# Attention with an MLP behind it: normalised rows of six batches transposed by DMA on ScalarE's queue instead of by TensorE

## The chip, the cores and the metric

One Trainium2 chip, one of its cores. The metric is the device time of one execution in microseconds; lower is better. It is given as the median of three runs.

## What is computed

Two stages, batch by batch. `q`, `k`, `v` are 8 batches x 8 heads x 576 rows x 64, `s` is 8 x 8 x 576.

```python
scores = scale * (q @ k.T) + min(-(cum[:, None] - cum[None, :]), 0)   # cum = cumsum(max(s, 0))
attn = softmax(where(causal, -1e9, scores))
x = (attn @ v), heads side by side                                    # 8 x 576 x 512
xn = (x - mean) / sqrt(var + 1e-6) * g_ln
out = x + max(xn @ w_ch1, 0) @ w_ch2                                  # 512 -> 2048 -> 512
```

## The kernel before, in words

The order of the work is written out by hand: every engine runs its instructions in program order, and the framework adds the semaphore waits that the data needs. The main loop runs over n = 0 to 63, one **slot** for each head h = n % 8 of each batch b = n // 8 (lines 745 to 834). The MLP is a `queue` of small **units** that the slots take from with `run_units`, so that TensorE has matmuls to do while other engines work on the attention.

A slot of the steady part (n from 16) does this, in this order:

- `pre(n)` (line 675): loads ahead. For batches 3 to 7, keys and queries come as rows: `ld_rows` (SP), `cast_rows` to bf16 with the bias columns beside them (POOL), and `tr_rows` (SP, line 186), a DMA transpose of up to 128 x 1024 elements into `kq`. For each half batch (4 heads) there are five `tr_rows`, issued by SP two, two and one in the slots h = 0, 1, 2 for the heads 4 to 7 of the batch and h = 4, 5, 6 for the heads 0 to 3 of the next. `ld_v` (SP, line 139) loads `v` of the next batch in slots h = 1 to 5, and `cast_v` (POOL) casts it a slot later.
- `scores(b, h)` (line 304): matmuls into three PSUM banks `sa`, `sb`, `sc` (pool `ps_s`, three buffers), and for each an exp on ScalarE into `er`; then four causal selects on POOL. The next slot's scores need those banks, so they wait for these exps. Even heads add `scores_d`.
- `run_units(1, True)`, `run_units(1)`, then `pv_next()`: the product with `v` for the head two slots before, and on VectorE its scaling into `xb` (and, for the last 64 rows, `xm`). In slot h = 1 it also finishes batch b - 1: `ln_open`, and `ln_xn` for each tile t, which writes a normalised tile `xn` (128 x 512, bf16; line 451). Tiles 0 to 3 are the batch's first 512 rows; tile 4 exists for odd batches only, and holds the last 64 rows of two batches.
- `ln_tr(b - 1, t)` for t = 0, 1 in slot h = 2 and t = 2, 3, 4 in slot h = 3: four TensorE transposes with the identity into PSUM (`trx`, line 484) and a copy by VectorE (by ScalarE for batch 1) into `xT`, or for tile 4 into `xTm`.
- the rest of the slot's units. At the end of slot h = 3 what is left of the queue is run and `batch_units(b - 1)` joins it: 16 units `mlp1` (line 493: four matmuls of 512 columns, then a relu into `hT`, by VectorE for the first unit of a slot and by ScalarE for the others), then 16 units `mlp2` (line 511: four matmuls each; four units finish one row tile, VectorE forms `yo` at line 524, and SP stores it at line 542). `nu` spreads them, four to a slot.

`ph` and `py` of the MLP share the pool `ps_m` with two buffers, `yo` has three, `xn` five, `xT` two (one for each of two batches).

After the loop comes a tail: the last two `pv`, the tiles of batch 7 one by one (`ln_xn`, a unit, `ln_tr` with a copy by ScalarE), the rest of batch 6's units, batch 7's units, and `mixed_units` for the 512 rows in `xm`.

The lines that the change and the working touch most:

```python
lt = {2: (0, 1), 3: (2, 3, 4)}.get(h, ()) if b > 1 else ()
for t in lt:
    ln_tr(b - 1, t, "act" if b == 2 else "dve")
    if t != 1 and t != 4:
        run_units(1)
        nu -= 1
...
if b > 1 and h == 3:
    run_units(len(queue))
    queue += batch_units(b - 1)
```

Of the kernel before, what the change touches and what calls it, by code (L numbers as in the profile page):

```python
# [15 lines left out]
P = 128  # L16
# [3 lines left out]
def kernel(  # L20
# [11 lines left out]
    nc = tc.nc  # L32
    B, H, S, D = q.shape
# [5 lines left out]
    NF = S // P  # L39
# [48 lines left out]
    xTm = const.tile([P, KD, 512], BF16, name="xTm")  # L88
# [7 lines left out]
    def copy_on(eng, out, in_):  # L96
        if eng == "act":
            nc.scalar.copy(out=out, in_=in_)  # L98
        elif eng == "dve":
            nc.vector.tensor_copy(out=out, in_=in_)  # L100
        else:
            nc.gpsimd.tensor_copy(out=out, in_=in_)  # L102
# [140 lines left out]
    def tr_pair(g):  # L243
        tr_kind("k", g)
        tr_kind("q", g)
# [58 lines left out]
    def scores(b, h):  # L304
        e = er[:, h % 4, :]
        pe_mask = b * H + h < NM

        def bank(name, blocks, o):
            a = ps_s.tile([P, 512], F32, name=name, tag="s")
            for c, kb, q0, q1, diag in blocks:  # L310
                for a0, a1, cols in q_cols(b, h, q0, q1):
                    nc.tensor.matmul(  # L312
                        a[:, c + a0 - q0 : c + a1 - q0],
                        lhsT=k_cols(b, h, kb),
                        rhs=cols,
                        start=True,
                        stop=not (pe_mask and diag),
                    )
                if pe_mask and diag:
                    nc.tensor.matmul(  # L320
                        a[:, c : c + P], lhsT=ident, rhs=maskT, start=False, stop=True
                    )
            nc.scalar.activation(out=e[:, o : o + 512], in_=a, func=ACT.Exp, scale=scale)  # L323

        bank("sa", ((0, 0, 0, 512, True),), 0)
        bank("sb", ((0, 0, 512, 576, False), (64, 1, 128, 576, True)), OB)
        bank("sc", ((0, 2, 256, 576, True), (320, 3, 384, 576, True)), OC)
        if pe_mask:
            return
        for o in (0, OB + 64, OC, OC + 320):  # L330
            nc.gpsimd.affine_select(  # L331
                out=e[:, o : o + P],
                in_=e[:, o : o + P],
                compare_op=ALU.is_ge,
                fill=0.0,
                base=0,
                pattern=[[1, P]],
                channel_multiplier=-1,
            )
# [70 lines left out]
    def x_tiles(b):  # L410
        ts_ = [xb[b][:, t, :] for t in range(NF)]
        if b % 2 == 1:
            ts_.append(xm[b // 2])
        return ts_
# [13 lines left out]
    xTs = {}  # L428
    xns = {}
# [5 lines left out]
    def ln_rstd(b):  # L435
        n = len(x_tiles(b))
        rs = rstd[:, b, 0:n]
        nc.vector.tensor_scalar_add(out=rs, in0=mvs[b][:, 0:n, 1], scalar1=1e-6)  # L438
        nc.gpsimd.tensor_tensor(out=rs, in0=rs, in1=mhalf[:, 0:n], op=ALU.pow)  # L439

    def ln_aggr(b, t):
        nc.vector.bn_aggr(out=mvs[b][:, t, :], in_=st[b][:, t, 0 : 4 if b == 0 else 3, :])

    def ln_xn(b, t):
        tiles = x_tiles(b)
        if t >= len(tiles):
            return
        if b > 0:
            ln_aggr(b, t)
        xn = xnp.tile([P, Dm], BF16, name="xn", tag="xn")  # L450
        nc.vector.scalar_tensor_tensor(  # L451
            out=xn,
            in0=tiles[t],
            scalar=mvs[b][:, t, 0:1] if b > 0 else mean0[:, t : t + 1],
            in1=gb,
            op0=ALU.subtract,
            op1=ALU.mult,
        )
        xns[b, t] = xn
        if b > 0 and t == len(tiles) - 1:  # L460
            ln_rstd(b)
# [16 lines left out]
    def ln_tr(b, t, eng="dve"):  # L478
        if (b, t) not in xns:
            return  # L480
        xn = xns.pop((b, t))
        tr = ps_t.tile([P, KD, P], BF16, name="trx", tag="tr")
        for kd in range(KD):
            nc.tensor.transpose(tr[:, kd, :], xn[:, kd * P : (kd + 1) * P], ident)  # L484
        if t < NF:
            dst = xTs[b][:, :, t * P : (t + 1) * P]
        else:
            dst = xTm[:, :, (b // 2) * P : (b // 2 + 1) * P]
        copy_on(eng, dst, tr)

    first_unit = [False]

    def mlp1(xT, fb):
# [63 lines left out]
    def run_units(n, dve_first=False):  # L557
        for i in range(n):
            if queue:
                first_unit[0] = dve_first and i == 0  # L560
                queue.pop(0)()
# [33 lines left out]
    for i in range(2):  # L595
# [5 lines left out]
        out=maskT,  # L601
        in_=maskT,
# [18 lines left out]
    for t in range(NT):  # L621
# [5 lines left out]
        out=c_in, in0=c_in, scalar1=0.0, scalar2=1.0 / scale, op0=ALU.max, op1=ALU.mult  # L627
    )
    nc.vector.tensor_tensor_scan(
        out=c_sc, data0=c_one, data1=c_in, initial=0.0, op0=ALU.mult, op1=ALU.add  # L630
# [114 lines left out]
    for n in range(BH):  # L745
        b, h = n // H, n % H
        pre(n)
        if n < 8:
            scores(b, h)
            if h in (1, 3, 5, 6):  # L750
                scores_d(b, h // 2)
            if h in (0, 2, 4):
                qk_pair(h // 2 + 1, ("dve", "dve"), ("act", "dve" if h < 4 else "act"))
            pend.append((b, h))
            if n == 7:
                pv_next()
                tr_pair(4)
                pv_next()
                evac_pair("k", 4, ("act", "act"))
                evac_pair("q", 4, ("act", "act"))  # L760
                trc = bias_tr()
                keep_warm(8)
                continue
            if n % 2 == 1 or n == 0:
                keep_warm(2)
            if n > 1:
                pv_next()
            if n == 6:
                pv_next()
            continue  # L770
        if n == 8:

            phs = [
                pool.tile([P, 512], F32, name="ph", tag=tag)
                for pool, tag in ((ps_m, "m"), (ps_m, "m"), (ps_s, "s"), (ps_s, "s"))
            ]

            def columns(t):
                cols = slice(t * P, (t + 1) * P)
                for fb, ph in enumerate(phs):  # L780
                    for kd in range(KD):
                        nc.tensor.matmul(  # L782
                            ph[:, cols],
                            lhsT=w1_bf[:, kd, fb * P : (fb + 1) * P],
                            rhs=xTs[0][:, kd, cols],
                            start=(kd == 0),
                            stop=(kd == KD - 1),
                        )

            for t in range(NF):  # L790
                ln_tr(0, t, "act" if t < 3 else "dve")
                if t > 0:
                    columns(t - 1)
            columns(NF - 1)
            for fb, ph in enumerate(phs):
                if fb % 2 == 0:
                    nc.scalar.activation(out=hT[:, fb, :], in_=ph, func=ACT.Relu)
                else:
                    nc.vector.tensor_scalar_max(out=hT[:, fb, :], in0=ph, scalar1=0.0)
            ln_first_rstd()  # L800
            queue += batch_units(0)[4:]
            scores(b, h)
            scores_d(b, h // 2)
            pend.append((b, h))
            run_units(1)
            continue

        end = next(m for m in (8 * i + 3 for i in range(2, B + 1)) if m >= n)
        nu = (2 if n < 16 else -(-len(queue) // (end - n + 1))) - 2
        if n in PAIRS:  # L810
            qk_pair(PAIRS[n], ("dve", "dve"), ("act", "act"))
        scores(b, h)
        run_units(1, True)
        if h % 2 == 0:
            scores_d(b, h // 2)
        run_units(1)
        if n > 9:
            pv_next()
        if n == 9:
            bias_rows(trc)  # L820
        pend.append((b, h))
        lt = {2: (0, 1), 3: (2, 3, 4)}.get(h, ()) if b > 1 else ()
        for t in lt:
            ln_tr(b - 1, t, "act" if b == 2 else "dve")
            if t != 1 and t != 4:
                run_units(1)
                nu -= 1
        if n == 2 * H + 2:
            for t in range(3, NT):
                ln_xn(1, t)  # L830
        run_units(nu)
        if b > 1 and h == 3:
            run_units(len(queue))
            queue += batch_units(b - 1)
    pv_next()
# [3 lines left out]
    for t in range(NT):  # L839
        ln_xn(B - 1, t + 1)  # L840
        run_units(1)
        ln_tr(B - 1, t, "act")
    run_units(len(queue))
    queue += batch_units(B - 1)
    queue += mixed_units()
# [30 lines left out]
```

## Time and profile before

| | |
|---|---|
| median of 3 runs | 368.11 us (367.84 to 368.29) |
| the profiled execution | 368.74 us, of which the span from first to last instruction is 367.0 us |
| TensorE busy | 357.8 us, 3079 matmuls |
| VectorE, ScalarE, POOL busy | 205.8, 194.2, 161.3 us |
| DMA transposes on SP's queue (`tr_rows`) | 50, 1274 ns in the middle from start to end of issue |
| TensorE transposes of `xn` (`trx`) | 144 |
| DMAs on ScalarE's queue | 5 stores, at the end |

In a profile line the first number is the start in us from the start of the span, the second the length in us; then the engine (PE is TensorE, ACT ScalarE, DVE VectorE, SPq SP's DMA queue), the line of the kernel, the operation, output <- input with shapes, and how many of them were merged. In brackets stands the idle time of the engine before it, and what ended that. A row for a DMA shows its issue on the queue, not its landing; landings are in the trace as events of the DMA's semaphore. In the answer for one tile the three numbers are the least, middle and greatest length in ns.

### The profile page before, as it was taken

How to read it: one execution, taken by the hardware profiler on the slowest of the kernel's cores; microseconds unless marked ns; L12 is line 12 of the kernel's file. 1: busy time of each engine (PE TensorE's matmuls, PEld its weight loads, DVE VectorE, ACT ScalarE, POOL GpSimd, SP SyncE). 2: the span in 40 equal slices, each digit the busy share in tenths (PEclk: the TensorE clock that was granted, in tenths of full speed). 3: DMA queues.
4: the chain of work that ended last, by engine and by line, in shares of the span. 5: the costliest groups of instructions: out<-in, count | busy, mean ns of one | idle time of the engine just before them, and what ended most of it. 6: DMA issues, size and time to landing. Idle time of an engine off the chain costs nothing.

```text
span 367.0 us, 8372 instructions
## 1 busy us (share of the span) xinstructions
PE 357.8 (97%) x3079; PEld 198.0 (54%) x3079; DVE 205.8 (56%) x539; ACT 194.2 (53%) x371; POOL 161.3 (44%) x441
## 2 busy tenths in 40 slices
PE   8899999999999999999999999999999999999995
PEld 3577565565555555555555555555555554444444
DVE  7597789796438453944384547743675483112211
ACT  5795988568743674357534753476337522501410
POOL 8864375747553746445754562555652101000000
PEclk9999999999999999999999999999999999999999
DMA  7999995579965989599968996798730011011013
GB/s 138 170 195 175 201 204 88 116 179 173 187 140 129 236 177 189 117 227 184 192 158 203 206 188 133 183 202 183 167 102 2 0 60 57 3 56 58 3 29 86
DMA packets 147981, 50.42 MB, mean 137 GB/s; under 512 B 134185, under 2 KB 143268, under 8 KB 147940
## 3 DMA queue, kind: packets, MB, share of 16 engines
q1 hardware_dynamic: 129364, 40.74, 50.9%
q0 software_dynamic: 18176, 8.62, 20.4%
q10 hardware_dynamic: 400, 0.52, 0.5%
q8 instruction: 24, 0.39, 0.4%
q14 instruction: 17, 0.14, 0.2%
HBM read 37.11 MB, written 9.44 MB: 127 GB/s over the span
## 4 chain that ended last, share of the span: by engine, by line
PE 85%; DVE 7%; ACT 3%; DMA 2%; issue 1%; ACTq 0%
PE ph L497 32%; PE py L515 31%; PE pot L389 7%; PE sc L312 4%; PE sa L312 3%; PE sb L312 3%; DVE xn L451 2%; PE trx L484 2%; ACT er L323 2%; DMA kq<-c 1%; ACT kq L98 1%; PE trqk L255 1%; DVE stats L423 1%; PE ph L782 1%; DMA c_in<-in_s_dram 1%
## 5 line engine op out<-in xcount | busy, mean ns | idle before, releaser
L515 PE MATMUL py<-w_bf,hT 128*128 128x512 bf16 (+1 forms) x592 | 136.5, 373 | 0.4 <-DVE yo L524 0.4
L497 PE MATMUL ph<-xT,w_bf 128*128 128x512 bf16 x496 | 117.8, 379 | 0.1
L507 ACT ACTIVATE hT<-ph 128x512 bf16<-128x512 f32 x102 | 61.0, 598 | 62.8 <-PE ph L497 62.8
L515 PEld LDWEIGHTS <-hT 128*128 128x128 bf16 x592 | 53.5, 98 | 49.1 <-issue 0.9
L497 PEld LDWEIGHTS <-w_bf 128*128 128x128 bf16 x560 | 50.3, 97 | 51.7 <-issue 3.3
L323 ACT ACTIVATE er<-sa 128x512 bf16<-128x512 f32 x64 | 38.2, 597 | 70.3 <-PE sa L312 39.9
L331 POOL TENSOR_SCALAR_AFFINE_SELECT er<-er 128x128 bf16<-128x128 bf16 x216 | 58.2, 294 | 26.4 <-ACT er L323 26.3
L505 DVE TENSOR_SCALAR hT<-ph 128x512 bf16<-128x512 f32 x38 | 26.3, 692 | 54.5 <-PE ph L497 49.1
L176 POOL CAST rows<-rowtmp 128x512 bf16<-128x512 f32 (+1 forms) x50 | 30.5, 609 | 49.1 <-DMA rowtmp<-in_q_dram 48.4
L312 PEld LDWEIGHTS <-kq 68*128 68x128 bf16 x440 | 32.8, 97 | 26.5 <-DMA kq<-c 1.6
L389 PEld LDWEIGHTS <-er 128*128 128x128 bf16 x960 | 37.4, 98 | 14.2 <-issue 0.7
L389 PE MATMUL pot<-v_bf,er 128*128 128x65 bf16 x960 | 39.6, 193 | 0.1
L323 ACT ACTIVATE er<-sc 128x512 bf16<-128x512 f32 x64 | 39.1, 610 | 0.0
L397 DVE RECIPROCAL rinv<-pot 128x5 f32<-128x5 f32 x64 | 12.3, 192 | 47.5 <-PE pot L389 47.2
L323 ACT ACTIVATE er<-sb 128x512 bf16<-128x512 f32 x64 | 38.3, 598 | 0.1
L524 DVE SCALAR_TENSOR_TENSOR yo<-py,rstd,xb 128x512 f32<-128x512 f32 x32 | 23.9, 748 | 25.5 <-PE py L515 20.8
L399 DVE TENSOR_TENSOR xb<-pot,rinv 128x256 f32<-128x256 f32 x64 | 27.2, 425 | 2.2
L439 POOL TENSOR_TENSOR rstd<-rstd,mhalf 128x4 f32<-128x4 f32 (+1 forms) x8 | 8.8, 1097 | 43.8 <-DVE rstd L438 43.8
L312 PE MATMUL sa<-kq 68*128 68x512 bf16 x64 | 24.4, 381 | 1.2 <-DMA kq<-c 1.1
L423 DVE BATCH_NORM_STATS2 stats<-xb 128x6 f32<-128x128 f32 (+2 forms) x100 | 25.3, 312 | 0.4
L312 PE MATMUL sc<-kq 68*128 68x256 bf16 (+1 forms) x208 | 25.2, 232 | 0.3
L102 POOL CAST v_bf<-vtmp 128x512 bf16<-128x512 f32 (+1 forms) x30 | 18.4, 613 | 14.3 <-DMA vtmp<-in_v_dram 14.3
(101 smaller groups left out, 332.8 us busy)
## 6 DMA issues: line engine op xcount, KB each, us to landing
out_dram<-yo SPq DMA_DIRECT2D x32, 256.0 KB
vtmp<-in_v_dram SPq DMA_DIRECT2D x24, 256.0 KB
rowtmp<-in_k_dram SPq DMA_DIRECT2D x40, 128.0 KB
rowtmp<-in_q_dram SPq DMA_DIRECT2D x40, 128.0 KB
w_bf<-in_moe_w_ch_dram POOLq DMA_DIRECT2D x8, 512.0 KB, 11.1
kp<-in_k_dram POOLq DMA_DIRECT2D x11, 144.0 KB, 6.6
qp<-in_q_dram POOLq DMA_DIRECT2D x11, 144.0 KB, 7.3
v_bf<-in_v_dram POOLq DMA_DIRECT2D x8, 128.0 KB, 8.5
```

Source lines behind the costliest of these rows:

```text
L176: nc.gpsimd.tensor_copy(out=r[0:pn, :, :, 0:D], in_=loaded.pop(("rows", gam, t))[0:pn])
L312: nc.tensor.matmul(a[:, c + a0 - q0 : c + a1 - q0], lhsT=k_cols(b, h, kb), rhs=cols, start=True, stop=not (pe_mask and diag),)
L323: nc.scalar.activation(out=e[:, o : o + 512], in_=a, func=ACT.Exp, scale=scale)
L331: nc.gpsimd.affine_select(out=e[:, o : o + P], in_=e[:, o : o + P], compare_op=ALU.is_ge, fill=0.0, base=0, pattern=[[1, P]], channel_mult ...
L389: nc.tensor.matmul(pot[:, t, :], lhsT=e[:, o : o + P], rhs=vv[:, kb, h, :], start=(kb == 0), stop=(kb == last),)
L399: nc.vector.tensor_tensor(out=xb[b][:, :, hs], in0=pot[:, 0:NF, 0:D], in1=rinv[:, 0:NF].unsqueeze(2).to_broadcast([P, NF, D]), op=ALU.mult,)
L423: nc.vector.bn_stats(out=st[b][:, t, part, :], in_=x[:, lo:hi])
L497: nc.tensor.matmul(ph, lhsT=w1_bf[:, kd, fb * P : (fb + 1) * P], rhs=xT[:, kd, :], start=(kd == 0), stop=(kd == KD - 1),)
L505: nc.vector.tensor_scalar_max(out=hT[:, fb, :], in0=ph, scalar1=0.0)
L507: nc.scalar.activation(out=hT[:, fb, :], in_=ph, func=ACT.Relu)
L515: nc.tensor.matmul(py[0], lhsT=hT[:, fb, t * P : (t + 1) * P], rhs=w2_bf[:, fb, c0:c1], start=(fb == 0), stop=(fb == FB - 1),)
L524: nc.vector.scalar_tensor_tensor(out=yo, in0=py[0], scalar=rs, in1=x[:, c0:c1], op0=ALU.mult, op1=ALU.add)
```

## The change

A new function `ln_dma(b, t)` transposes an `xn` tile by one DMA transpose, issued on ScalarE's queue, straight into `xT` or `xTm`. It takes the place of `ln_tr` for batches 2 to 7; batches 0 and 1 keep `ln_tr`. In the loop it is called at these places, for batch b - 1:

- t = 0 in slot h = 2, t = 2 in slot h = 3 and t = 4 in slot h = 5, each after `pv_next()` and ahead of the slot's remaining units;
- t = 1 in slot h = 3 and t = 3 in slot h = 4, each after `pre(n)` and ahead of `scores(b, h)`.

In the tail it replaces `ln_tr` for batch 7. The units of batch b - 1 now join the queue at the end of slot h = 4 instead of h = 3, and `end`, from which `nu` is worked out, moves by one slot with it.

```diff
--- before.py
+++ after.py
@@ -487,6 +487,16 @@
         else:
             dst = xTm[:, :, (b // 2) * P : (b // 2 + 1) * P]
         copy_on(eng, dst, tr)
+
+
+    def ln_dma(b, t):
+        if (b, t) not in xns:
+            return
+        if t < NF:
+            dst = xTs[b][:, :, t * P : (t + 1) * P]
+        else:
+            dst = xTm[:, :, (b // 2) * P : (b // 2 + 1) * P]
+        nc.scalar.dma_start_transpose(out=dst, in_=xns.pop((b, t)))
 
     first_unit = [False]
 
@@ -805,8 +815,10 @@
             run_units(1)
             continue
 
-        end = next(m for m in (8 * i + 3 for i in range(2, B + 1)) if m >= n)
+        end = next(m for m in (8 * i + 4 for i in range(2, B + 1)) if m >= n)
         nu = (2 if n < 16 else -(-len(queue) // (end - n + 1))) - 2
+        if b > 2 and h in (3, 4):
+            ln_dma(b - 1, 2 * h - 5)
         if n in PAIRS:
             qk_pair(PAIRS[n], ("dve", "dve"), ("act", "act"))
         scores(b, h)
@@ -819,17 +831,19 @@
         if n == 9:
             bias_rows(trc)
         pend.append((b, h))
-        lt = {2: (0, 1), 3: (2, 3, 4)}.get(h, ()) if b > 1 else ()
+        lt = {2: (0, 1), 3: (2, 3, 4)}.get(h, ()) if b == 2 else ()
         for t in lt:
-            ln_tr(b - 1, t, "act" if b == 2 else "dve")
+            ln_tr(b - 1, t, "act")
             if t != 1 and t != 4:
                 run_units(1)
                 nu -= 1
         if n == 2 * H + 2:
             for t in range(3, NT):
                 ln_xn(1, t)
+        if b > 2 and h in (2, 3, 5):
+            ln_dma(b - 1, {2: 0, 3: 2, 5: 4}[h])
         run_units(nu)
-        if b > 1 and h == 3:
+        if b > 1 and h == 4:
             run_units(len(queue))
             queue += batch_units(b - 1)
     pv_next()
@@ -839,7 +853,7 @@
     for t in range(NT):
         ln_xn(B - 1, t + 1)
         run_units(1)
-        ln_tr(B - 1, t, "act")
+        ln_dma(B - 1, t)
     run_units(len(queue))
     queue += batch_units(B - 1)
     queue += mixed_units()
```

## The prediction

> **What bounds the kernel now.** I read the page first, parts 1, 2 and 4: busy time, slices, the chain that ended last.
>
> ```profile
> PE 357.8 (97%) x3079; PEld 198.0 (54%) x3079; DVE 205.8 (56%) x539; ACT 194.2 (53%) x371; POOL 161.3 (44%) x441
> PE   8899999999999999999999999999999999999995
> PE 85%; DVE 7%; ACT 3%; DMA 2%; issue 1%; ACTq 0%
> ```
>
> TensorE has no slice with room in it, and the chain lies on it: a matmul taken away is time saved, a pause of TensorE is time lost. Then the answer for the tile trx, which the change removes from batch 2 on:
>
> ```profile
> L484 PE MATMUL trx<-ident,xn x144: 217/219/230, 32.1 to 303.1; 128*128 128x128 bf16 x144
> L100 DVE COPY xT<-trx x21: 403/415/425, 35.6 to 271.7; 128x512 bf16<-128x512 bf16 x21
> ```
>
> 219 ns is a latency. What four transposes cost TensorE is read from starts in the timeline; lines from slots 42 and 43 (batch 5, h = 2 and 3), and the next pair of SP's own transposes:
>
> ```profile
> 186.13 0.38 PE L312 MATMUL sa<-kq 68*128 68x512 bf16 x1
> 188.06 0.27 ACT L358 ACTIVATE er<-sd 64x128 bf16<-64x128 f32 x1
> 189.04 0.39 PE L484 MATMUL trx<-ident,xn 128*128 128x128 bf16 x4
> 189.26 1.03 PE L515 MATMUL py<-w_bf,hT 128*128 128x512 bf16 x4
> 190.02 0.74 DVE L524 SCALAR_TENSOR_TENSOR yo<-py,rstd,xb 128x512 f32<-128x512 f32 x1
> 190.79 0.36 SPq L542 DMA_DIRECT2D out_dram<-yo  x1
> 191.24 1.22 SPq L186 DMA_TRANSPOSE kq<-rows  x1
> 191.69 0.60 ACT L323 ACTIVATE er<-sa 128x512 bf16<-128x512 f32 x1 [3.36 <-PE sb L312]
> 194.78 0.51 SPq L139 DMA_DIRECT2D vtmp<-in_v_dram  x1
> 200.72 3.15 SPq L186 DMA_TRANSPOSE kq<-rows  x2
> ```
>
> The reader is to see three things. Four transposes take 189.26 - 189.04 = 0.22 us. ScalarE is done with slot 42 at 188.33 and idle for 3.36 us. And SP's transposes fall between: the one that slot 42 issues in program order starts only at 191.24, because SP stood behind a store that waited for yo, which VectorE computes after four xn.
>
> The trace's semaphore records give landings: SP's 50 transposes land 2.65 to 5.52 us after they start, median 3.38; the ten of 64 rows (as many elements as an xn tile) 2.65 to 2.94.
>
> **What the Trainium skill says.** "DMA: Bandwidth & Descriptors", section "Silent corruption: two transposing streams in flight at once": transposes issued from SP and from ACT are two streams, and the first of the later stream must wait for the full completion of the earlier. Before, only SP transposes, so no run here shows it; the forecast rests on the changed program keeping this order both ways. "Perfetto Trace Analysis", section "DMA Instruction — HWDGE (DVE, Sync)": the reported time of a DMA leaves out its semaphore wait and the movement of data. The trace agrees: 1.27 us reported, 3.38 us to landing. "TensorE: Matmul & The Clock Gate", section "What's actually happening": after an idle window of some 3.4 us the array runs at half rate. The trace agrees at the start, where 12 matmuls of 512 columns take 5.13 us (0.43 each; 0.216 later).
>
> **The change, part by part.** Slots are counted from the scores of one head to those of the next; plain ones last 4.58 or 4.63 us.
>
> Removed, TensorE: 4 full tiles for each of 6 batches and 3 mixed tiles, 27 groups of four. Slots h = 2 and 3 last 5.08 and 5.03 us (5.62 where the batch being normalised is odd), so 0.45 + 0.45 or 0.45 + 1.04 over plain ones: 3 x 0.90 + 2 x 1.49 = 5.7 us in the loop. In the tail five groups at 0.22 are 1.1. Together **-6.8 us**. The 22 copies of VectorE (415 ns) and 5 of ScalarE (587 ns) lie beside TensorE: nothing.
>
> Added, issue: 27 DMAs. No ScalarE transpose is in the trace; nearest are SP's of 64 rows, 1.22 to 1.27 us. I take 1.25, not less than the 0.5 us of a plain DMA there, not more than SP's longest 2.43. 27 x 1.25 = 34 us of ScalarE, but in slots with only exps (ScalarE busy 1.72 of 4.64 us in slot 42), so without waits it costs nothing. It cannot gain, since it only adds to the queue.
>
> Moved: the MLP chunk one slot later. Four units of 0.86 us go from the loop to the tail, where TensorE is as full: 0, within 1 us either way. It keeps tile 3's landing before its first reader, and covers the tail: eight units (6.9 us) stand between the last transposes of batch 7 and their reader.
>
> Added, waits. Behind ln_dma on ScalarE stand the exps of the next slot; behind these the next-but-one scores, which need the score banks (three, one per sa, sb, sc). I count from the start of slot h = 2.
> - T0 (tile 0) comes after SP's last row transpose of that slot. That lands at +7.7, 9.2, 7.8, 9.4, 8.3 us in batches 3 to 7; ScalarE is there at +2.2. T0 starts at the landing.
> - T1 comes next, before the exps of h = 3. Here a second wait: SP's and ScalarE's DMAs use eight semaphores in turn, and in the records none is issued before the DMA eight places back has landed (on GpSimd's eight, several are issued 0.28 us after, i.e. were waiting). Eight back from T1 is SP's v load of slot h = 2 (194.78 above), landing at +11.8, 14.2, 12.8, 13.6; batch 7 has none. T1 starts there.
> - So the exps of h = 3 start at S = T1 + 1.25: +13.1, 15.5, 14.1, 14.9 and, in batch 7, 10.8. They take 1.6 us and the scores of h = 4 end 0.4 later, at S + 2.05; undisturbed they end at 4.63 + 4.58 + 0.9 = +10.1. Stalls 5.0, 7.4, 6.0, 6.8, 2.7: **+28 us**.
> - T2 starts when those exps end. SP's two row transposes of h = 4 must wait until it lands (2.75), the second starts 1.3 later and lands after 3.3; T3, written before the exps of h = 4, waits for that; then 1.25 issue, 1.65 exps, 0.4 scores: 10.65 us, of which 5.0 are a slot in any case. 5.65 each in batches 3 to 6: **+22.6 us**. Bounds 5.2 to 7 each: the two transposes took 4.7 to 6.5 us from first start to last landing. In batch 7 SP has none left.
> - T4 (batches 4 and 6) waits likewise for SP's next pair; two relus stand behind it, about 1.2 us each: **+2.4**.
> - SP also waits for T2, T3 and T4; loads behind it slip by 3 us, which the longer slots cover. POOL's casts wait for those loads and have the same cover.
> - Half rate after a stall: 0 to +10. What follows the first stall is hidden in the second; I take **+2**.
>
> Sum: -6.8 + 28 + 22.6 + 2.4 + 2 = +48. The profiled execution is 368.74 us (span 367.0 and 1.7 around it): 417. The median shown is 0.6 lower: **416 us**.
>
> **Rivals.**
> - Only the cross-queue wait; the turn of eight semaphores does not hold ScalarE. Then T1 follows T0, the first stalls are 2.1, 3.7, 2.3, 3.8, 2.7 (14.6 us), the rest as above: -6.8 + 14.6 + 22.6 + 2.4 + 1 = +34, about 402. For it: SP's own DMAs never show such a wait. Against: GpSimd's do.
> - Deeper stalls, with half rate after most of them and SP's lag growing from batch to batch: 8 to 15 us more, about 428. Against: between stalls SP has longer slots to catch up.
> - The other side: the transposes of the two queues do not hold each other, since they are apart in time or the program does not order them. Then 368.1 - 6.8, about 361.5. For it: ScalarE has the room, and the data has a slot to land. It decides at one point: SP's transpose of slot h = 2 must have landed when ScalarE reaches T0, at +2.2. In the trace it lands at +7.7 or later in all five batches, since SP stands behind the store of yo.
> - The DMA transposes might be split so that the change does not do what it says. With 128 x 512 tiles of 2-byte elements, half of what SP issues whole, I see no reason.
>
> **How the numbers follow.** Forecast 0.57; cross-queue wait alone 0.22; deeper stalls 0.08; queues not holding each other 0.10; hidden down to within 0.2% 0.03. What a measurement can tell from no change is about 0.2%. Faster 0.10, same 0.03, slower 0.87. The forecast's own range is 407 to 426 (4 x 1.4 for SP's pair, 8 for half rate, 3 for the landings); with the cross-queue case and part of the deeper one, 394 to 430.
>
> **What would show it.** In the changed profile: no trx after batch 1, 27 transposes on ScalarE's queue of about 1.25 us; ScalarE idle before T0 until SP's landing, before T1 until the v load, before T3 until SP's pair; TensorE idle before sa of h = 4 (3 to 7 us) and of h = 5 (5 to 6 us) in batches 3 to 6, and only before h = 4 in batch 7; SP's row transposes of h = 4 and 5 right after ScalarE's landings. It is wrong if TensorE stays at 97% and the time falls; if ScalarE does not idle before T1, the second wait is wrong; if the stall at h = 5 is missing, T3's place is.

## The result, and the profile after

The changed kernel takes **397.04 us** in the median of 4 runs (392.22 to 400.33), the kernel before on the same chip 368.20 (367.84 to 368.85): ratio 1.0738, 95% interval [1.0637, 1.0838], 28.8 us slower. 416 was forecast, 394 to 430 as the range. The run at 400.33 counts as a slow one, and the ratio is of the three fast runs alone, so it lies a little below 397.04 / 368.20. The profiled execution of the changed kernel took 397.96 us, its span is 396.3.

The page of the changed kernel, parts 1, 2, 4 and 5 (PEclk is the clock granted to TensorE, in tenths):

```profile
PE 362.1 (91%) x2971; PEld 194.0 (49%) x2971; DVE 197.4 (50%) x516; ACT 192.6 (49%) x367; POOL 165.7 (42%) x441
PE   8999999999998999597996998958998999999996
PEclk9999999999999999979999899998999999999999
PE 23%; DMA 1%; DVE 0%; ACT 0%; issue 0%
L507 PE MATMUL ph<-xT,w_bf 128*128 128x512 bf16 x496 | 122.8, 390 | 14.3 <-DMA rowtmp<-in_q_dram 5.9
```

TensorE has 108 instructions less, the 27 groups of four, and is idle for 396.3 - 362.1 = 34.2 us, where before it was 367.0 - 357.8 = 9.2. That is 25.0 us of the 29.3 that the span grew. The other 4.3 are more busy time with fewer instructions: the clock of TensorE falls to half three times (the 7 and the two 8 in PEclk). The chain is followed back only over the last quarter, so it says nothing of batches 3 to 7; waits and timelines have to. Ahead of the first MLP matmuls (ph) TensorE idles 14.3 us, where before it was 0.1; the line of the page before (the last number is the idle time):

```profile
L497 PE MATMUL ph<-xT,w_bf 128*128 128x512 bf16 x496 | 117.8, 379 | 0.1
```

The answers for the tiles trx and xT, with least, middle and greatest length in ns:

```profile
L484 PE MATMUL trx<-ident,xn x36: 219/219/230, 31.8 to 81.3; 128*128 128x128 bf16 x36
```

```profile
L499 ACTq DMA_TRANSPOSE xT<-xn x24: 1204/1252/1627, 109.4 to 328.7; - x24
```

From batch 2 on no trx is left, and an issue on ScalarE takes 1.25 us, as taken. Now the timeline of batch 4, from the end of slot h = 2 (scores at 148.16) to slot h = 7; DMA rows and TensorE's waits:

```profile
152.05 2.53 ACTq L499 DMA_TRANSPOSE xT<-xn  x2
155.88 1.21 SPq L186 DMA_TRANSPOSE kq<-rows  x1
158.69 2.56 ACTq L499 DMA_TRANSPOSE xT<-xn  x2
168.23 3.57 PE L507 MATMUL ph<-xT,w_bf 128*128 128x512 bf16 x8 [4.32 <-DMA rowtmp<-in_q_dram]
170.19 7.99 SPq L186 DMA_TRANSPOSE kq<-rows  x2
174.44 1.21 ACTq L499 DMA_TRANSPOSE xTm<-xn  x1
180.88 3.26 SPq L186 DMA_TRANSPOSE kq<-rows  x2
185.98 1.26 SPq L186 DMA_TRANSPOSE kq<-rows  x1
188.11 0.39 PE L312 MATMUL sa<-kq 68*128 68x512 bf16 x1 [1.37 <-DMA kq<-rows]
```

To be read with the landings from the trace's semaphore records:

```
tiles 0, 1    ScalarE 152.05, 153.30   landed 154.38, 155.82
SP, h = 2     SP      155.88           landed 158.62
tiles 2, 3    ScalarE 158.69, 159.97   landed 165.41, 167.98
SP, h = 4, a  SP      170.19           landed 174.37
tile 4        ScalarE 174.44           landed 176.81
SP, h = 4, b  SP      176.94           landed 180.02
```

From the second row on, each change of stream but one starts 0.06 to 0.14 us after the landing of the other stream. So the two streams do hold each other, and the waits are in the program: ahead of its transpose at 155.88 SP waits for the semaphores of tiles 0 and 1. At the one change left (170.19) SP is held in another way: two of the loads ahead of it, issued at 165.42 and 168.00, waited for tiles 2 and 3 to land, because each uses the semaphore of the DMA eight places back (the turn of eight semaphores of the prediction). But look at the order: tiles 0 and 1 go **ahead** of SP's transpose of slot h = 2, not behind it, tiles 2 and 3 go ahead of the pair of h = 4, not between, and tile 4 goes into the middle of that pair. The MLP's first unit starts 0.25 us after tile 3 has landed; the profile names a load ("rowtmp"), which ended near it, where the landing of xT is meant. And from 180.88 on SP's last three row transposes run late, and the scores at 188.11 wait for them.

The waits on SP's queue for ScalarE's transposes (L186 is SP's transpose; L164 and L139 are loads, held by the turn of the semaphores), and TensorE's waits, over the whole span (us in total, times, longest):

```profile
SPq L186 <- DMA xTm<-xn: 10.5, 2, 5.3
SPq L164 <- DMA xT<-xn: 10.2, 6, 3.0
SPq L186 <- DMA xT<-xn: 8.7, 4, 3.2
SPq L139 <- DMA xT<-xn: 3.6, 2, 1.8
```

```profile
PE ph L507 <- DMA rowtmp<-in_q_dram: 5.9, 2, 4.3
PE sb L312 <- DMA kq<-rows: 4.4, 4, 1.6
PE ph L507 <- issue: 4.2, 2, 2.4
PE ph L507 <- ACT hT L517: 4.2, 2, 3.6
PE pot L389 <- POOL er L331: 2.9, 2, 1.9
PE py L525 <- DVE yo L534: 1.9, 2, 1.1
```

No scores wait for an exp of ScalarE; that wait, on which both large terms of the forecast rested, is not in the list at all. What TensorE waits for is xT (ph), a relu behind tile 4 (ph for hT), SP's row transposes (kq), selects of POOL (pot), and yo of VectorE (py).

Slots longer than plain ones (4.58 or 4.63 us), counted from scores to scores in batches 3 to 7 and summed by place:

| slots | forecast | measured | of which, by batch 3, 4, 5, 6, 7 |
|---|---|---|---|
| h = 3 and 4 | 28 | 5.7 | 0.3, 1.1, 1.8, 1.3, 1.3 |
| h = 5 | 22.6 | 15.1 | 1.9, 7.25, 4.2, 1.7, 0 |
| h = 6 | 2.4 | 5.8 | 0, 0.8, 0, 5.0, 0 |
| h = 7 and the next h = 0 | 0 | 8.7 | 1.8, 4.1, 0, 2.8 |
| sum | 53 (and 2 for half rate) | 35.3 (up to 5.9 of it half rate) | |

Before, the slots h = 2 and 3 were 5.7 us over plain ones; 35.3 - 5.7 is +29.6. Ahead of batch 3 the loop is 2.8 us shorter and after the last slot's scores 2.3 longer, since four MLP units moved there and five groups of transposes went. Together that is 29.1; the span grew by 29.3, the median by 28.8. The half rate is an estimate: TensorE is busy for 11.8 us of the three stretches, and half of that is 5.9.

### The profile page after: what moved, and what is told of

Same layout as the page of the kernel before. It is cut to its first block, busy times and chain, and to the rows that moved or that the text cites. A ratio compares the mean times of both kernels' runs of the same rounds, so it can differ in the third digit from the quotient of the medians.

```text
span 396.3 us, 8238 instructions
## 1 busy us (share of the span) xinstructions
PE 362.1 (91%) x2971; PEld 194.0 (49%) x2971; DVE 197.4 (50%) x516; ACT 192.6 (49%) x367; POOL 165.7 (42%) x441
## 5 line engine op out<-in xcount | busy, mean ns | idle before, releaser
L507 PE MATMUL ph<-xT,w_bf 128*128 128x512 bf16 x496 | 122.8, 390 | 14.3 <-DMA rowtmp<-in_q_dram 5.9
L525 PE MATMUL py<-w_bf,hT 128*128 128x512 bf16 (+1 forms) x592 | 134.1, 373 | 1.9 <-DVE yo L534 1.9
L507 PEld LDWEIGHTS <-w_bf 128*128 128x128 bf16 x560 | 51.5, 99 | 69.6 <-issue 21.4
L331 POOL TENSOR_SCALAR_AFFINE_SELECT er<-er 128x128 bf16<-128x128 bf16 x216 | 60.4, 304 | 23.2 <-ACT er L323 23.1
L389 PEld LDWEIGHTS <-er 128*128 128x128 bf16 x960 | 38.4, 99 | 19.3 <-POOL er L331 4.4
L389 PE MATMUL pot<-v_bf,er 128*128 128x65 bf16 x960 | 41.8, 195 | 3.1 <-POOL er L331 2.9
L312 PE MATMUL sb<-kq 68*128 68x64 bf16 (+1 forms) x168 | 24.5, 246 | 4.9 <-DMA kq<-rows 4.4
## 6 DMA issues: line engine op xcount, KB each, us to landing
rowtmp<-in_k_dram SPq DMA_DIRECT2D x40, 128.0 KB
rowtmp<-in_q_dram SPq DMA_DIRECT2D x40, 128.0 KB
v_bf<-in_v_dram POOLq DMA_DIRECT2D x8, 128.0 KB, 8.4
```

What stands on the lines that cost most here:

```text
L312: nc.tensor.matmul(a[:, c + a0 - q0 : c + a1 - q0], lhsT=k_cols(b, h, kb), rhs=cols, start=True, stop=not (pe_mask and diag),)
L331: nc.gpsimd.affine_select(out=e[:, o : o + P], in_=e[:, o : o + P], compare_op=ALU.is_ge, fill=0.0, base=0, pattern=[[1, P]], channel_mult ...
L389: nc.tensor.matmul(pot[:, t, :], lhsT=e[:, o : o + P], rhs=vv[:, kb, h, :], start=(kb == 0), stop=(kb == last),)
L507: nc.tensor.matmul(ph, lhsT=w1_bf[:, kd, fb * P : (fb + 1) * P], rhs=xT[:, kd, :], start=(kd == 0), stop=(kd == KD - 1),)
L525: nc.tensor.matmul(py[0], lhsT=hT[:, fb, t * P : (t + 1) * P], rhs=w2_bf[:, fb, c0:c1], start=(fb == 0), stop=(fb == FB - 1),)
```

## The experiments

All ratios are to the kernel before, run beside on the same chip (368.19 to 368.49 us). Diffs are against the changed kernel unless said otherwise.

**Is it the two streams?** e1 puts the tiles on SP's queue, e2 makes their DMAs plain copies, e7 makes SP's DMAs plain copies and keeps ScalarE's transposes. e2 and e7 leave transposition out, so what they compute is not the result.

```diff
-        nc.scalar.dma_start_transpose(out=dst, in_=xns.pop((b, t)))
+        nc.sync.dma_start_transpose(out=dst, in_=xns.pop((b, t)))
```

> The changed kernel with the 27 transposes of xn issued by SP in the same places instead of by ScalarE: one transposing stream, and no DMA wait stands ahead of an exp or a relu. Theory (the loss is the order of two transposing streams, and ScalarE and SP standing in it): near the time without the TensorE transposes, 361 to 367 us. Rival 1 (the DMA transpose of xn lands too late because it shares the DMA engines with the row loads, 4 to 8 us in the changed profile): the stalls ahead of the first MLP units stay, 372 to 380 us. Rival 2 (SP's queue is full and row loads get late): 370 to 385 us, with waits for kq ahead of scores.

Measured: 417.88 us (417.41 to 419.17), ratio 1.1343 [1.1306, 1.1381]: a miss, slower still. One queue has no stream to wait for, but its own order. Timeline of e1, batch 4:

```profile
172.88 3.25 SPq L499 DMA_TRANSPOSE xT<-xn  x2
176.87 2.67 SPq L186 DMA_TRANSPOSE kq<-rows  x2
181.57 1.25 SPq L499 DMA_TRANSPOSE xT<-xn  x1
184.69 3.59 PE L507 MATMUL ph<-xT,w_bf 128*128 128x512 bf16 x8 [13.14 <-DMA xT<-xn]
```

And TensorE's waits in e1:

```profile
PE ph L507 <- DMA xT<-xn: 46.0, 4, 13.1
```

Tile 3 stands on SP behind the row pair, loads and a store, and goes out at 181.57; the MLP's first unit needs it and idles 13.14 us. Four such waits are 46.0 us. SP's lag, which the forecast knew for h = 2, is the bound here; e1 therefore doesn't clear the streams, it only shows what SP's own queue costs.

```diff
-        nc.scalar.dma_start_transpose(out=dst, in_=xns.pop((b, t)))
+        nc.scalar.dma_start(
+            out=dst, in_=xns.pop((b, t)).rearrange("p (k c) -> p k c", k=KD)
+        )
```

> The changed kernel with each DMA transpose of xn replaced by a plain DMA copy of the same tile on ScalarE's queue: the transposition of these tiles is left out. The waits that keep two transposing streams apart go, the turn of the eight DMA semaphores, the issue on ScalarE and the traffic stay. Theory (order of the streams): 361 to 368 us. Rival 1 (traffic: late landings) and rival 3 (the turn of eight semaphores, SP's loads waiting for ScalarE's DMAs): 372 to 395 us, with SP waiting for xT ahead of row loads as in the changed kernel (10.2 us there).

Measured: 369.43 us (367.04 to 373.67, 20 runs), ratio 1.0032 [1.0009, 1.0054], a little above the theory's upper end. The same tiles on the same queue at the same places, and 27.6 of 28.8 us are gone. Its SP queue has no wait for xT, and its copies land in 2.2 to 3.8 us, but for one of 5.1.

The edit of e7 at its main line (not shown: the shapes behind it, and lines that zero the bias columns and leave out the VectorE copies that fill them in slot n = 9):

```diff
-        nc.sync.dma_start_transpose(
+        nc.sync.dma_start(
...
```

> The changed kernel with SP's 50 row transposes replaced by plain DMA copies of the same rows (their transposition is left out, and the bias columns are zero): ScalarE's 27 transposes are real and the only transposing stream. Theory (order of two streams): 366 to 374 us. Rival (a transpose on ScalarE's queue lands late because it runs among SP's loads, whatever the order): the landings of tiles 2 and 3 stay at 4 to 8 us and the stalls ahead of h = 5's first unit stay, 376 to 390 us.

Measured: 364.01 us (363.81 to 364.95), ratio 0.9894 [0.9875, 0.9913]. ScalarE's 27 transposes are all there, and the kernel is 4.2 us **faster** than before. So neither ScalarE's issue nor the DMA transpose as such costs TensorE anything here; 33 us go when SP's side no longer transposes. This is an upper figure: SP's plain issue is shorter as well (0.54 us in the middle, 1.27 before), which relieves SP, though its rows land no sooner (3.5 us in the middle, 3.4 before). What is left of TensorE's waits from batch 3 on is yo:

```profile
PE py L528 <- DVE yo L537: 1.3, 2, 0.7
```

The loss goes with the transposition on either side, and the trace shows the waits, so the meeting of two transposing streams is its cause. What isn't tested apart is how it acts: SP waits 19.2 us with its transposes for ScalarE's and 13.8 us with its loads, by the turn of the semaphores, for the same late tiles. The turn by itself costs little: e2 and e7 keep it.

**What does the later MLP chunk cost?** e4 is the kernel before with the chunk one slot later, e10 with two slots; nothing else. Diff against the kernel before (for e10, 5 in the place of 4):

```diff
-        end = next(m for m in (8 * i + 3 for i in range(2, B + 1)) if m >= n)
+        end = next(m for m in (8 * i + 4 for i in range(2, B + 1)) if m >= n)
...
-        if b > 1 and h == 3:
+        if b > 1 and h == 4:
```

> The kernel before with the MLP chunks beginning one slot later and nothing else. All theories: 0, within 1 us of before (367 to 369 us), since TensorE is full in the loop and in the tail alike. If it is more than 1 us off, the shift is a term of its own in the sum.

Measured: 371.03 us (369.83 to 371.70, 10 runs), ratio 1.0061 [1.0041, 1.0081]: +2.8, where 0 was forecast. From TensorE's waits in e4 between 90 and 340 us:

```profile
PE sb L312 <- DMA kq<-rows: 1.0, 2, 0.6
```

From the scores of the last slot to the end, e4 takes 3.7 us more (four units of 0.86 are 3.4); from n = 16 to that slot only 0.9 less. In batch 2 it gains 2.4: the queue is empty in slot h = 4, and TensorE's transposes of q there wait 0.9 us with no unit to cover it. From batch 3 on it loses 1.5, most of it where the scores of h = 0 in batches 5 and 6 wait for rows. In batch 4 a store now stands on SP between the two pairs of row transposes (at 166.89), where before there was none.

> The kernel before with the MLP chunks beginning two slots later and nothing else: the control of the run before. The shift by one slot cost 2.8 us. Theory (the cost is single waits of scores for kq, since SP's row transposes now stand behind stores that come later): 369 to 373 us. If it is 368.2 or less, the shift by one was an accident of where the stores fall; if it is over 374, the shift is a term that grows with its length.

Measured: 373.09 us (371.58 to 373.51), ratio 1.0112 [1.0077, 1.0146]: +4.6, just over what was expected, but not by the waits that were expected: no scores wait for rows in its profile. After the scores of the last slot e10 takes 7.1 us more, and from n = 16 to there only 2.2 less, since TensorE runs out of units in batch 2. It idles 1.2 us ahead of the scores of h = 6 there, and then runs at half rate for 3.41 us.

**What does tile 4's place cost?** In e3 TensorE transposes tile 4 of batches 3 and 5, in e5 its DMA goes out right behind tile 3 (the diff is that of e5):

```diff
             ln_dma(b - 1, 2 * h - 5)
+            if h == 4:
+                ln_dma(b - 1, 4)
...
-        if b > 2 and h in (2, 3, 5):
-            ln_dma(b - 1, {2: 0, 3: 2, 5: 4}[h])
+        if b > 2 and h in (2, 3):
+            ln_dma(b - 1, {2: 0, 3: 2}[h])
```

> The changed kernel with tile 4 in the loop (batches 3 and 5 normalised, slot h = 5 of batches 4 and 6) transposed by TensorE again. Tiles 0 to 3 stay on ScalarE's queue. Theory: the stream changes fall from four to two in these batches, no relu stands behind a DMA wait, and SP's next row transposes go out in one piece: 12 us less, about 385 us (slots h = 5 to 7 of batches 4 and 6 lose some 16 us in the changed profile, of which the wait for tile 3 ahead of h = 5's first unit stays). Rival 1 (late landings alone): within 3 us of the changed kernel, 394 to 400 us.

> The changed kernel with tile 4 issued on ScalarE's queue directly behind tile 3 (slot h = 4) instead of in slot h = 5: the same 27 transposes on ScalarE, two stream changes a batch fewer in batches 4 and 6, and no relu behind a DMA wait. Theory (the place between SP's row transposes is what costs, not the DMA): near the run with tile 4 on TensorE, 383 to 388 us. Rival (each transpose on ScalarE's queue costs what it costs): 394 to 400 us as the changed kernel.

Measured: e3 384.29 us (382.68 to 385.11), ratio 1.0421 [1.0381, 1.0460]; e5 385.65 us (382.69 to 386.01), ratio 1.0455 [1.0424, 1.0486]. Both as their theory had it: two DMAs in the middle of SP's pairs cost 11.4 to 12.7 us, and it is their place, since e5 has as many DMAs as the changed kernel. In the profiles most of it lies in slots h = 5 and 6 of batches 4 and 6 (14.8 us over plain slots in the changed kernel, 6.8 in e3, 5.7 in e5), little in late rows for the next batch (6.9, 5.3 and 5.4 in h = 7 and the next h = 0). But the changed profile is 5.0 us behind that of e3 by the end of slot h = 5 of batch 4 (counted from batch 3), when its first tile 4 has only just gone out, so one profile of each does not show how the whole 12 come about.

**Fewer changes of stream.** A visit is one stretch of ScalarE's transposes between SP's. e6 sends tiles 0 to 3 together in slot h = 2 (tile 4 by TensorE), e9 all five together in h = 3, with the chunk two slots later. Not shown in the diffs are the calls in h = 3 and 4 that go, and in e9's those in h = 2, 3 and 5 and the lines of the chunk.

```diff
-        if b > 2 and h in (2, 3, 5):
-            ln_dma(b - 1, {2: 0, 3: 2, 5: 4}[h])
+        if b > 2 and h == 2:
+            for t in range(NF):
+                ln_dma(b - 1, t)
+        if b > 2 and h == 5:
+            ln_tr(b - 1, 4, "dve")
```

> Tiles 0 to 3 all issued by ScalarE at the end of slot h = 2, in one piece; tile 4 on TensorE in slot h = 5; MLP chunks as in the changed kernel. One visit of ScalarE's stream per batch instead of two, and none of its transposes in flight with the row loads that SP issues behind its own transpose. Theory: tile 3 lands long before h = 5, so the 1.5 to 2.5 us ahead of the first MLP unit and the half rate behind it go; SP's transpose of h = 2 waits some 5 us longer and its loads with it: 376 us (372 to 380), with the remaining loss at scores that wait for kq. Rival (the wait of SP is the whole cost): 385 us or more.

Measured: 388.16 us (387.13 to 389.94), ratio 1.0546 [1.0517, 1.0575]: a miss, in the range of the rival, and slower than e3 with its two visits. Timeline of e6, batch 4:

```profile
152.03 5.49 ACTq L499 DMA_TRANSPOSE xT<-xn  x4
158.90 1.20 SPq L186 DMA_TRANSPOSE kq<-rows  x1
161.61 0.61 PE L312 MATMUL sb<-kq 68*128 68x64 bf16 x3 [2.94 <-DMA kq<-rows]
```

The first MLP unit no longer waits, as expected. But SP's row transpose of slot h = 2 has a reader as near, the scores of slot h = 4, and it now waits for four tiles (last landing 158.72) in the place of two. Those slots last 8.3 to 11.5 us in place of 4.63. Half rate adds to it: the clock record of e6 has 20.5 us of it between batch 3 and the tail, that of e3 10.2.

```diff
+        if b > 2 and h == 3:
+            for t in range(NT):
+                ln_dma(b - 1, t)
```

> All tiles of a batch (tile 4 too) issued by ScalarE in one piece at the end of slot h = 3, in the gap between SP's fifth row transpose of one half batch and the first pair of the next; MLP chunks begin two slots later than before, in h = 6. 27 DMA transposes as in the changed kernel, one visit a batch. Theory (what counts is which of SP's transposes with a near reader has to wait, not the number of DMAs): 368 to 376 us, with little waiting for kq at h = 4 and nothing ahead of the first MLP unit; the slot's exps stand behind 5 or 6 us of issue, which may cost 1 to 2 us a batch. Rival (any second stream costs about what it costs in the grouped run, since SP stands for the visit wherever it lies): 380 to 390 us.

Measured: 380.08 us (377.04 to 382.17), ratio 1.0295 [1.0246, 1.0345]: a miss as well, at the lower end of the rival. It is 7.0 over its control e10, although TensorE has 27 groups of transposes less. No stall over 0.3 us is left at h = 4 or ahead of the first MLP unit; but SP's row transposes wait until all tiles of the batch have landed, and the scores of the next h = 0 for them (from TensorE's waits in e9 between 90 and 340 us):

```profile
PE sb L312 <- DMA kq<-rows: 3.9, 4, 1.2
PE sa L312 <- DMA kq<-rows: 2.4, 2, 1.5
```

**A version that gains.** e8 keeps TensorE's transposes in the loop and uses the DMA in the tail only, where SP transposes nothing; e11 also for tiles 0 to 3 of batch 6, which come up in batch 7, where SP transposes no rows after h = 2, with that one chunk a slot later. Diff of e8 against the kernel before, beside the new function:

```diff
-        ln_tr(B - 1, t, "act")
+        ln_dma(B - 1, t)
```

> The kernel before with the DMA transposes on ScalarE's queue in the tail alone (batch 7, five tiles), where SP has no row transposes left and ScalarE has nothing else to do. The loop is as before. All theories: 1.1 us less than before, 366.8 to 367.5 us, five groups of transposes at 0.22 us. No gain would mean that something in the tail takes the place of the removed matmuls.

Measured: 367.36 us (366.74 to 367.81, 19 runs), ratio 0.9967 [0.9951, 0.9983], as expected, though 0.8 us less in place of 1.1. Timeline of e8:

```profile
294.73 10.09 PE L525 MATMUL py<-w_bf,hT 128*128 128x512 bf16 x46
296.67 5.84 ACTq L499 DMA_TRANSPOSE xT<-xn  x4
```

TensorE runs without a break over the four transposes. It has the lowest median of the kernels here that do the whole work, by the interval 0.2 to 0.5% under the kernel before.

> The kernel before with the tail by DMA on ScalarE and, in the loop, batch 6 alone by DMA: its four tiles at the end of slot h = 3 of batch 7, behind SP's very last row transpose, with that one MLP chunk a slot later (TensorE transposes stay in batches 2 to 5). ScalarE's stream waits once and nothing of SP's comes behind it. Theory: 0.9 us under the run with the tail alone, 366.0 to 366.9 us. Rival (a visit costs 2 us or more wherever it lies): 368 to 370 us.

Measured: 367.56 us (366.76 to 372.97, 22 runs), ratio 0.9972 [0.9955, 0.9990]: no better than the tail alone, a miss. In its profile the tiles of batch 6 land 4.7 to 6.9 us after issue, with only two stores and no load beside them, and TensorE waits 0.35 us for an exp and 0.6 for xT in slots h = 4 and 5 of batch 7. The profiled run took 369.73, 2.2 us over the median, so whether this gives back the gain in the others is open.

## Why the prediction was right in its sign and too high

By the runs, the changed kernel without the second transposing stream takes 364.0 us (e7), 4.2 less than before. The other 33 belong to two streams that meet, as an upper figure; e2 has 27.6. The forecast had 55 for its stalls and half rate.

- **"Together -6.8": mis-sized.** In e7 the slots from batch 3 to the last are 3.9 us shorter than before, in place of 5.7. Most of the rest lies in slot h = 3 of batches 4 and 6. The forecast took their 1.04 over a plain slot for transposes, but 0.8 stays: TensorE then waits for yo (0.65 and 0.66 us), which VectorE forms only after xn. In the tail e8 has 0.8 in place of 1.1.
- **Issue on ScalarE at no cost: right.** It takes 1.25 us, and in e7 no wait of TensorE from batch 3 on is for ScalarE.
- **The streams hold each other, both ways: right**, and it carries the sign. This is the rule of the Trainium skill, "DMA: Bandwidth & Descriptors", section "Silent corruption: two transposing streams in flight at once". The trace agrees: a stream goes out 0.06 to 0.14 us after the other's landing in batch 4.
- **"T0 (tile 0) comes after SP's last row transpose of that slot": failed.** This is the step that made the forecast too high. The order across two queues was read from the order of the source. In the trace T0 follows SP's transposes of slot h = 1: it starts at +2.1, 3.9, 4.5, 3.05 and 4.05 us from the start of h = 2 (forecast +7.7 to 9.4), and SP's last transpose waits for T1 instead. So no scores wait for ScalarE's exps. The 5.7 us in the place of the 28 are other waits: 2.7 for rows and 1.9 for yo among them.
- **"T1 comes next ... Here a second wait": failed.** T1 follows T0 by 1.24 to 1.30 us in batches 4 to 7. The turn of the eight semaphores is real, but SP has it: its loads wait for xT (L164, 10.2 us, and L139, 3.6), and six are issued 0.016 us after the landing eight places back.
- **"T3, written before the exps of h = 4, waits for that": failed in mechanism.** T2 and T3 go out together ahead of SP's pair. A stall at h = 5 is there nonetheless, 15.1 in place of 22.6, since tile 3 lands late: 8.0 us after its issue in batch 4 and 5.5 to 6.2 in batches 3, 5 and 6, where 2.75 was taken. That figure came from a trace without ScalarE's DMAs beside SP's loads (and one of its ten landings was at 3.03, not under 2.94).
- **T4, +2.4: mis-sized.** The relu behind T4 holds TensorE 3.55 us in batch 6 and 0.6 in batch 4, the mechanism as told. But SP's second of the pair waits for T4 too, and the whole place costs about 12 (e3, e5).
- **"SP also waits ... which the longer slots cover. POOL's casts ... have the same cover": failed.** In h = 7 and the next h = 0 TensorE waited 3.1 us for rows and 2.9 for selects of POOL; these stood behind a cast of v, whose load came late on SP's queue. In all, these slots lost 8.7 us.
- **The shift, 0: wrong** by itself, +2.8 (e4). What it costs within the changed kernel is not known: e7 has the shift too, and none of e4's waits for rows.
- **Half rate, +2: mis-sized.** The clock record has one stretch of 6.83 us and two of 3.41 at half rate; by the estimate above they cost up to 5.9.

The range held the time, close to the rival of 402 us, but for other reasons than either gave, and so in good part by luck: the errors in the first stall (-22) and the second (-7.5) were partly made up by T4, SP's lag and half rate. How the 33 us split between late tiles, late rows, the turn of the semaphores and half rate isn't settled, as each stretch changes with the others: e5 has one half-rate stretch, e3 three, with nearly the same time.

## What to carry to other kernels

A DMA transpose on a second queue cost nothing by itself here (e7, e8); it costs at the changes between the streams, where the next transpose waits for a landing, and with it all that its queue holds. So ask for each stream which reader comes next and how near: grouping only moved the wait to SP's rows (e6, e9), and the one place that gained has no other stream (e8). Taking work from a full engine also gains less than its length where the work had covered another wait, as the transposes had covered part of the wait for yo. The order in which two queues follow each other must be read from the built program or a trace, not from the lines of the source.

## What the runs showed of the hardware

- In the changed kernel, batches 3 to 6, tiles 2 and 3, behind which SP's loads go out, land 4.2 to 8.0 us after their issue; in batch 7, where no loads follow, they land in 2.4 to 2.5, and tiles 0 and 1 and the tail's in 2.3 to 3.5. But loads are not all: the 4.7 to 6.9 us in e11 come with two stores alone.
- Transfers can stand still for a while. In the changed kernel some 20 packets of 256 bytes, of SP's and of ScalarE's queue, that begin between 160.66 and 161.09 us take 1.8 to 2.2 us each, while tiles 2 and 3 are under way; in e11 others take 2.3 to 3.0 from 270.46 on. The trace of the kernel before has such a case too (25 packets from 128.0 on, up to 1.4 us). What stops them is open.
- The Trainium skill, "TensorE: Matmul & The Clock Gate", section "What's actually happening", speaks of an idle window of some 3.4 us before half rate. In e10 less was enough by the trace: its longest idle time in the loop from n = 16 on is 1.21 us, up to 86.00, and from 87.66 on matmuls of 512 columns take 631 ns in place of 379. In e9 the same gap had the same effect, while one of 2.21 us in e5 (up to 209.87) had none. TensorE in e10 by windows (length; busy time; granted clock; DMA share; GB/s):

```profile
84.00:86.00 2.00, 0.79 (x19) 1.00 0.79 156
86.00:88.00 2.00, 1.72 (x7) 0.89 0.59 135
88.00:92.00 4.00, 4.00 (x28) 0.63 1.18 215
```

The clock record there has a single stretch of 3.41 us at half rate, and in all runs the stretches between the start and the last few us are of 3.41 us or a multiple of it, up to 13.65. How much idleness within a window brings half rate on, the runs don't settle.
